# Signs of weights on another engine, first stores from another queue, the seven-product first layer one unit earlier

## The chip, the cores and the metric

The kernel runs on one core of a Trainium2 chip. The metric is device time in microseconds (us) of one execution. The engines are the tensor engine (PE, with its weight loads as PEld), the vector engine (DVE), the scalar engine (ACT), GpSimd (POOL) and the sync engine (SP), which here only issues DMA transfers.

## The reference

Four batches of 768 tokens go through an attention of 8 heads with 64 columns each. A token sees the 96 tokens up to itself and the first 8 of its batch, with a bias that falls with the distance by a slope of the head. Its result, 3072 tokens of 512 columns, goes through two dense layers with a PReLU between them:

```python
scores = scale * (q @ k.T) + bias          # per head
scores = where(is_global | is_local, scores, -1e9)
a = softmax(scores)                        # rows sum to 1
x = (a @ v) -> 3072 x 512                  # heads side by side
h = x @ w_in                               # 512 -> 2048
g = maximum(h, 0) + alpha * minimum(h, 0)
out = g @ w_out                            # 2048 -> 512
```

## The kernel before

The 3072 tokens are 12 units u of 256 tokens (`NU`, `UT`), three to a batch. The 2048 hidden columns are 16 blocks f of 128 (`NF`). All dense products have f32 accuracy from f16 pairs: each operand is a high part and a rest, and three matmuls (high x high, high x rest, rest x high) replace one.

*Weights.* They come as 64-bit floats. `split_w` (L464 to 492) turns each of the 16 blocks, in two parts of 512 columns (of `w_in` and of `w_out`), into f32 and then into an f16 pair. Per part: ACT scales the high word by 2^-112 into `wf`, which moves the exponent (L473, by the helper `mul`, L343); DVE shifts that left by 3 into `wb` (L479); DVE takes the sign bit from the raw word and joins it (L482); DVE joins the top bits of the low word into `wf` (L485); ACT writes the f16 high part (L488), DVE the rest (L363).

*Attention* (`attend`). Scores are 64-row matmuls, softmax is on DVE and ACT. Units 0 and 1 run in plain f32 with PE transposes; from unit 2 on transposes go through DMA, and from unit 4 on (`QU`) the scores are f16 products as well, for which `scale_bias` (L554) rescales the 8 bias tiles `D` on ACT.

*First layer.* `ff_in2` (L853) serves units under `US`: for each block 12 matmuls of 256 columns (L876, 4 column blocks times 3), a scaling by alpha (`g`, ACT, L343), and for each two blocks the maximum on DVE (L885), the f16 high part on ACT (L887) and the rest on DVE (L362). `ff_in4` (L780) serves units from `US` on, for four blocks at a time: a 2x2 scheme of seven instead of eight block products, each 12 matmuls of 128 columns for each of two column halves, into three banks X, Y and Z (L809). ACT takes intermediate sums out of the banks (L817), DVE joins them (L820, L837), applies PReLU (L845) and writes the rest (L362), ACT the high part (L852). It needs four sums of input blocks per unit (`x_combine`, L743, in the names `t` and `xs`) and sums of weights (`combine_w`, L495, in the names `ws` and `sw`).

*Second layer.* `ff_out` (L890) adds block f with three matmuls of 512 columns for each of the two 128-token tiles t (L907). After f = 15 ACT evacuates the tile into `os` (L918) and SP stores it. `os` lies in the tag `stage`, which has two buffers. The two tiles of unit 1 are accumulated in the banks of the tags `sp` and `ax`, which the attention needs too.

*Order.* Every operation has a key (16 slots per unit, L945 to 980) and one or two engines that could do it. A planner (`Plan`, L140) simulates all engines with costs from simple formulas, gives each operation to an engine and writes one queue per engine; tags with a few buffers limit how far it runs ahead. So one changed number moves operations everywhere. The engines execute their queues strictly in order.

A last branch to a general path is taken only for inputs outside the checked bounds; it doesn't run here. Squares of inputs and weights (`energy`, L432) feed that check.

## Time and profile before

| | |
|---|---|
| median of three runs | 608.42 us (608.40 to 608.44) |
| profiled execution | 608.45 us |
| its span in the trace | 606.7 us, 1.75 us less than its time |
| PE busy | 589.6 us, 97% |
| DVE busy | 508.4 us, 84% |
| ACT busy | 409.5 us, 68% |
| mean granted clock of PE | 0.993 |

The span runs from the first instruction to the last. A busy time counts every stretch in which the engine works on some instruction. Instructions of one engine overlap a little at their ends, so the distance of two starts says more of a price than one duration does. The granted clock is a share of 2.4 GHz.

### The profile page before, as it was taken

How to read it: one execution, taken by the hardware profiler on the slowest of the kernel's cores; microseconds unless marked ns; L12 is line 12 of the kernel's file. 1: busy time of each engine (PE TensorE's matmuls, PEld its weight loads, DVE VectorE, ACT ScalarE, POOL GpSimd, SP SyncE). 2: the span in 40 equal slices, each digit the busy share in tenths (PEclk: the TensorE clock that was granted, in tenths of full speed). 3: DMA queues.
4: the chain of work that ended last, by engine and by line, in shares of the span. 5: the costliest groups of instructions: out<-in, count | busy, mean ns of one | idle time of the engine just before them, and what ended most of it. 6: DMA issues, size and time to landing. Idle time of an engine off the chain costs nothing.

```text
span 606.7 us, 15901 instructions
## 1 busy us (share of the span) xinstructions
PE 589.6 (97%) x6218; PEld 416.1 (69%) x6218; DVE 508.4 (84%) x1367; ACT 409.5 (68%) x1088; POOL 1.6 (0%) x11
## 2 busy tenths in 40 slices
PE   8999999998999899999999999999999999999995
PEld 6776576656656666777777777777777777776772
DVE  7999999998999998899889879879788788764531
ACT  7986787885666756869579679668477677542421
POOL 1000000000000000000000000000000000000000
PEclk9999999998999999999999999999999999999998
DMA  8996233347525344557558748648847627313001
GB/s 314 412 409 219 96 111 102 68 119 178 136 76 138 100 119 108 151 117 141 134 96 152 144 97 145 139 80 142 131 107 151 156 66 115 90 27 44 37 1 40
DMA packets 133938, 78.97 MB, mean 130 GB/s; under 512 B 114912, under 2 KB 116960, under 8 KB 133856
## 3 DMA queue, kind: packets, MB, share of 16 engines
q1 hardware_dynamic: 133568, 77.63, 52.4%
q8 instruction: 50, 0.82, 0.6%
q14 instruction: 32, 0.26, 0.1%
q10 hardware_dynamic: 288, 0.26, 0.1%
HBM read 43.79 MB, written 6.29 MB: 83 GB/s over the span
## 4 chain that ended last, share of the span: by engine, by line
PE 75%; DVE 19%; ACT 3%; issue 2%; DMA 1%; ACTq 0%; DVEq 0%
PE o L907 33%; PE hx L809 14%; PE hy L809 7%; PE h L876 7%; PE av L691 4%; PE hz L809 4%; PE sp L610 3%; PE sp L617 2%; DVE g L885 2%; DVE pr L633 2%; DVE gg L362 2%; DVE wf L485 1%; DVE whl L363 1%; DVE wb L482 1%; ACT pr L638 1%
## 5 line engine op out<-in xcount | busy, mean ns | idle before, releaser
L907 PE MATMUL o<-whl,ghl 128*128 128x512 f16 (+1 forms) x774 | 193.8, 378 | 0.0
L809 PEld LDWEIGHTS <-sw 128*128 128x128 f16 x1536 | 93.4, 98 | 20.8
L638 ACT ACTIVATE pr<-pr,sm 128x256 f32<-128x256 f32 (+1 forms) x192 | 92.5, 484 | 20.7 <-DVE sm L633 20.7
L907 PEld LDWEIGHTS <-ghl 128*128 128x128 f16 x774 | 67.1, 98 | 55.2 <-issue 5.1
L876 PE MATMUL h<-xt,whl 128*128 128x256 f16 x768 | 93.2, 276 | 4.5 <-ACT g L343 3.2
L907 PE MATMUL o<-whl,gg 128*128 128x512 f16 x384 | 92.8, 380 | 1.6 <-DVE gg L362 1.3
L876 PEld LDWEIGHTS <-whl 128*128 128x128 f16 x768 | 75.0, 99 | 23.8 <-issue 7.3
L809 PEld LDWEIGHTS <-whl 128*128 128x128 f16 x1152 | 71.0, 98 | 18.9 <-issue 0.2
L633 DVE CUSTOM_DVE_ANT_0 pr<-sp,D 128x256 f32<-128x256 f32 (+1 forms) x192 | 70.1, 397 | 12.0 <-PE sp L610 10.8
L817 ACT ACTIVATE g<-hx 128x256 f32<-128x256 f32 x96 | 36.5, 380 | 59.9 <-PE hx L809 59.6
L845 DVE SCALAR_TENSOR_TENSOR hs<-hs,alpha 128x256 f32<-128x256 f32 x128 | 58.4, 480 | 18.1 <-ACT hs L817 17.3
L907 PEld LDWEIGHTS <-gg 128*128 128x128 f16 x384 | 35.2, 98 | 41.4 <-DVE gg L362 5.1
L363 DVE SCALAR_TENSOR_TENSOR ps<-pr,ps 128x512 f16<-128x512 f32 (+1 forms) x80 | 51.2, 644 | 5.9 <-ACT ps L343 5.7
L362 DVE TENSOR_TENSOR ghl<-hs,ghl 128x512 f16<-128x512 f32 x64 | 42.1, 686 | 2.2 <-ACT ghl L852 2.1
L852 ACT CAST ghl<-hs 128x512 f16<-128x512 f32 x64 | 36.8, 611 | 2.4 <-DVE hs L845 2.4
L638 ACT ACTIVATION_READ_ACCUMULATOR pr<-pr,sm 128x1 f32 x192 | 36.6, 190 | 0.0
L343 ACT ACTIVATE ps<-pr 128x512 f16<-128x512 f32 (+1 forms) x58 | 34.8, 600 | 0.9
L343 ACT ACTIVATE g<-h,ak 128x256 f32<-128x256 f32 x58 | 27.0, 466 | 10.8 <-PE h L876 9.9
L691 PEld LDWEIGHTS <-vp 128*128 128x128 f16 x888 | 30.4, 98 | 3.1 <-issue 0.4
L691 PE MATMUL av<-vp 128*128 128x64 f16 x888 | 32.4, 193 | 0.0
L817 ACT ACTIVATE hs<-hx 128x256 f32<-128x256 f32 x32 | 12.1, 379 | 29.1 <-PE hx L809 29.0
L363 DVE SCALAR_TENSOR_TENSOR vp<-v,vp 128x256 f16<-128x256 f32 (+1 forms) x80 | 31.3, 397 | 0.0
(134 smaller groups left out, 860.4 us busy)
## 6 DMA issues: line engine op xcount, KB each, us to landing
w<-in_w_dram SPq DMA_DIRECT2D x32, 512.0 KB, 8.5
qk<-in_qk_dram SPq DMA_DIRECT2D x28, 336.0 KB, 3.6
v<-in_vw_dram SPq DMA_DIRECT2D x28, 256.0 KB, 3.6
out_dram<-os SPq DMA_DIRECT2D x22, 256.0 KB, 3.5
qk<-in_qk_dram SPq DMA_DIRECT2D x12, 272.0 KB, 3.0
v<-in_vw_dram SPq DMA_DIRECT2D x12, 192.0 KB, 3.3
first<-in_first_dram SPq DMA_DIRECT2D x4, 464.0 KB, 4.7
first<-in_first_dram SPq DMA_DIRECT2D x4, 336.0 KB, 10.0
```

The source lines that it names most:

```text
L343: lambda: nc.scalar.mul(out=out(), in_=src(), mul=by.t if tile_ else by)),
L362: return e.tensor_tensor(out=out(), in0=src(), in1=hi(), op=ALU.subtract)
L363: return e.scalar_tensor_tensor(out=out(), in0=src(), scalar=val(), in1=hi(), op0=ALU.mult, op1=ALU.subtract)
L633: op("DVE", key, c_dve(n) + 10, lambda qb=qb, n=n, dc=dc, pc=pc: v.tensor_tensor_reduce(out=pr.t[:, pc : pc + n], in0=sp.t[:, pc : pc + n] ...
L638: op("ACT", key + 1, c_act(n, ptr=1) + 93, lambda qb=qb, n=n, pc=pc: nc.scalar.activation(out=pr.t[:, pc : pc + n], in_=pr.t[:, pc : pc + ...
L691: nc.tensor.matmul(out, lhsT=p_[:, 128 * j : 128 * j + 128], rhs=v_[:, 64 * j : 64 * j + 64], start=m == 0, stop=m == len(ps) - 1)
L809: nc.tensor.matmul(bank.t[:, 128 * q : 128 * q + 128], lhsT=wt(q, wi, c), rhs=xp(xi, c), start=begin and q == n == 0, stop=n == 5, skip_gr ...
L817: op("ACT", k, c_act(UT, True), lambda: nc.scalar.mul(out=out(), in_=two(bank), mul=KG), r=[bank], w=w, spare=SPARE if u < NU - 1 else 0)
L845: op("DVE", ks[4 + 2 * i], c_dve(UT, ptr=True), lambda n=n: v.scalar_tensor_tensor(out=hs.t[:, n, :], in0=hs.t[:, n, :], scalar=alpha[:, 4 ...
L852: op("ACT", ks[6], c_act(512), lambda q=q, cols=cols: nc.scalar.copy(out=ghl.t[:, 0, cols], in_=flat(q)), r=src, w=[(ghl, q)])
L876: nc.tensor.matmul(hp.t[:, cols], lhsT=w.t[:, wi, wc], rhs=x.t[:, NC * xi + c, :], start=n == 0, stop=n == 3 * NC - 1)
L907: nc.tensor.matmul(o.t[:, cols], lhsT=g_()[:, tok], rhs=w.t[:, wi, 512 + cols.start : 512 + cols.stop], start=f == 0 and n == 0, stop=f == ...
```

## The change

The diff below is whole. In words:

- `US` is 3 instead of 4: unit 3's first layer runs through `ff_in4` and its input through `x_combine`.
- For f from `SIGN` = 6 on, ACT makes the signs: it scales the raw high word once more by 2^-112 into f16, written to every second half-word of a buffer of zeros (`sg`, two of them in the tag `qs`, zeroed once by POOL). What is left of a scaled number at f16 is its sign. DVE then shifts `wf` left and joins `sg` in one instruction, so that the separate shift (L479) goes. For f under 6 the old instructions stay, with the second one writing to `wf`.
- Squares of inputs go to a buffer of the tag `pt` instead of `stage`.
- The 8 bias scalings are spread over slots instead of standing at one.
- The stores of units 0 and 1 are issued by ACT instead of SP.
- In the last unit and block only the second tile is cut into two halves.

```diff
--- before.py
+++ after.py
@@ -307,8 +307,9 @@
 WL = 3
 WLEAD = 8
 WARM = 9
-US = 4
+US = 3
 QU = 4
+SIGN = 6
 QLEAD = 2
 EV = 2
 SLEAD = 36
@@ -429,9 +430,9 @@
 
         en = cn["energies"]
 
-        def energy(key, src, r, col, n):
-
-            t = buf("gg" if n == 512 else "stage", f"sq{col}", [P, n], F16)
+        def energy(key, src, r, col, n, tag="stage"):
+
+            t = buf("gg" if n == 512 else tag, f"sq{col}", [P, n], F16)
             op("ACT", key, c_act(n) + 190, lambda: nc.scalar.activation(
                 out=t.t, in_=src(), func=AF.Square, accum_out=en[:, col : col + 1]), r=r, w=[t, (EN, col)])
 
@@ -455,6 +456,14 @@
             op("PE", key, 150, lambda: nc.tensor.matmul(
                 row.t[:, :NE], lhsT=cn["ones"], rhs=en, start=True, stop=True), r=[EN], w=[row])
             op("DVE", key, 1500, lambda: cn["check"](row.t[:, :NE]), r=[row])
+
+        signs = []
+
+        def clear_signs(key):
+            for i in range(2):
+                x = buf("qs", f"sg{i}", [P, 1344], F16)
+                op("POOL", key, 1500, lambda x=x: nc.gpsimd.memset(x.t, 0.0), w=[x])
+                signs.append(x)
 
         def load_w(f, key):
             raww[f] = [buf(raw_tag(), f"w{f}_{part}", [P, 1024]) for part in range(2)]
@@ -468,7 +477,7 @@
             n = 512
             for part, raw in enumerate(raww[f]):
                 w = buf("wf", f"wf{f}_{part}", [P, n])
-                bits = buf("wb", f"wb{f}_{part}", [P, n], I32)
+                sg = signs[(2 * f + part) % len(signs)]
                 cols = slice(n * part, n * part + n)
                 words = lambda raw=raw: raw.t.bitcast(I32).rearrange("p (n t) -> p n t", t=2)
                 lo_ = lambda words=words: words()[:, :, 0]
@@ -476,15 +485,24 @@
                 k = key + 0.01 * part
                 by = (WI, WO)[part]
                 mul(k, lambda w=w: w.t, lambda hi_=hi_: hi_().bitcast(F32), 2.0**-112, [raw], [w], n=n)
-                op("DVE", k, c_dve(n, True), lambda w=w, bits=bits: v.tensor_scalar(
-                    out=bits.t, in0=w.t.bitcast(I32), scalar1=3, scalar2=None, op0=ALU.logical_shift_left),
-                    r=[w], w=[bits])
-                op("DVE", k, c_dve(n), lambda bits=bits, hi_=hi_: v.scalar_tensor_tensor(
-                    out=bits.t, in0=hi_(), scalar=-0x80000000, in1=bits.t, op0=ALU.bitwise_and,
-                    op1=ALU.bitwise_or), r=[raw], w=[bits])
-                op("DVE", k, c_dve(n), lambda w=w, bits=bits, lo_=lo_: v.scalar_tensor_tensor(
-                    out=w.t.bitcast(I32), in0=lo_(), scalar=29, in1=bits.t, op0=ALU.logical_shift_right,
-                    op1=ALU.bitwise_or), r=[raw, bits], w=[w])
+                if f < SIGN:
+                    bits = buf("wb", f"wb{f}_{part}", [P, n], I32)
+                    op("DVE", k, c_dve(n, True), lambda w=w, bits=bits: v.tensor_scalar(
+                        out=bits.t, in0=w.t.bitcast(I32), scalar1=3, scalar2=None, op0=ALU.logical_shift_left),
+                        r=[w], w=[bits])
+                    op("DVE", k, c_dve(n), lambda w=w, bits=bits, hi_=hi_: v.scalar_tensor_tensor(
+                        out=w.t.bitcast(I32), in0=hi_(), scalar=-0x80000000, in1=bits.t, op0=ALU.bitwise_and,
+                        op1=ALU.bitwise_or), r=[raw, bits], w=[w])
+                else:
+                    op("ACT", k, c_act(n), lambda sg=sg, hi_=hi_: nc.scalar.mul(
+                        out=sg.t[:, : 2 * n].rearrange("p (n t) -> p n t", t=2)[:, :, 1], in_=hi_().bitcast(F32), mul=2.0**-112),
+                        r=[raw], w=[sg])
+                    op("DVE", k, c_dve(n), lambda w=w, sg=sg: v.scalar_tensor_tensor(
+                        out=w.t.bitcast(I32), in0=w.t.bitcast(I32), scalar=3, in1=sg.t[:, : 2 * n].bitcast(I32),
+                        op0=ALU.logical_shift_left, op1=ALU.bitwise_or), r=[sg], w=[w])
+                op("DVE", k, c_dve(n), lambda w=w, lo_=lo_: v.scalar_tensor_tensor(
+                    out=w.t.bitcast(I32), in0=lo_(), scalar=29, in1=w.t.bitcast(I32), op0=ALU.logical_shift_right,
+                    op1=ALU.bitwise_or), r=[raw], w=[w])
                 op("ACT", k, c_act(n), lambda w=w, by=by, cols=cols: nc.scalar.mul(
                     out=out.t[:, 0, cols], in_=w.t, mul=by), r=[w], w=[(out, part)])
                 rest(k, lambda cols=cols: out.t[:, 1, cols], lambda w=w: w.t, by,
@@ -738,7 +756,7 @@
                  [(y, 2 + qb)], 512)
 
         def x_energy(u, key):
-            energy(key, lambda: xt[u].t[:, :NC, :].rearrange("p c t -> p (c t)"), [xt[u], (whl[NF - 1], 3)], 2 * NF + u, 1024)
+            energy(key, lambda: xt[u].t[:, :NC, :].rearrange("p c t -> p (c t)"), [xt[u], (whl[NF - 1], 3)], 2 * NF + u, 1024, "pt")
 
         def x_combine(u, key):
 
@@ -894,7 +912,7 @@
                 acc[u] = [buf(("sp", "ax")[t] if u == 1 else "o", f"o{u}_{t}", [P, 512]) for t in range(2)]
             for t in range(2):
                 o = acc[u][t]
-                parts_ = 2 if u == NU - 1 and f == NF - 1 else 1
+                parts_ = 2 if t and u == NU - 1 and f == NF - 1 else 1
                 n_ = 512 // parts_
                 s = buf("stage", f"os{u}_{t}", [P, 512]) if f == NF - 1 else None
                 rows = u * UT + 128 * t
@@ -920,7 +938,7 @@
                     else:
                         op("DVE", key, c_dve(n_), lambda o=o, s=s, cols=cols: v.tensor_scalar(
                             out=s.t[:, cols], in0=o.t[:, cols], scalar1=OSC, scalar2=None, op0=ALU.mult), r=r, w=[z])
-                    on = nc.scalar if parts_ > 1 and part == 0 else nc.sync
+                    on = nc.scalar if u < 2 or parts_ > 1 and part == 0 else nc.sync
                     store = lambda on=on, s=s, rows=rows, cols=cols: on.dma_start(
                         out=a["out"][rows : rows + 128, cols], in_=s.t[:, cols])
                     if on is nc.sync:
@@ -947,12 +965,12 @@
         def begin(u):
             return 16 * u - LEAD - 2 if u > 2 else (-LEAD0, -LEAD1, 32 - LEAD2)[u]
 
-        jobs = [(-100, build_bias, ()), (-100, warm, ()), (slot(NU - 1, 6), check, ())]
+        jobs = [(-99, clear_signs, ()), (-100, build_bias, ()), (-100, warm, ()), (slot(NU - 1, 6), check, ())]
         for h in range(0, H, 2):
             jobs.append((-90, load_first, (0, h)))
             jobs.append((-60 + h / 8 if h else -71, load_first, (1, h)))
         for h in range(H):
-            jobs.append((begin(QU) - 0.5, scale_bias, (h,)))
+            jobs.append((begin(QU) + 2 * h - 3, scale_bias, (h,)))
         for u in range(NU):
             for h in range(H):
                 jobs.append((begin(u) + (2 if u else 1) * h, attend, (u, h)))
```

Three places show how the queues move. The rows are an engine's queue in order, with line, operation, output and inputs; the numbers behind a name are unit, part and a buffer's running number.

The first place is ACT's queue where the weights of blocks 7 to 9 are split, at about 60 us; before:

```order
L343 ACTIVATE wf7_0_905<-w7_0_480 128x512
L488 ACTIVATE whl5_881<-wf5_1_782 128x512
L343 ACTIVATE g1_1_889<-h1_1_861,ak_153 128x256
L343 ACTIVATE wf7_1_938<-w7_1_554 128x512
L488 ACTIVATE whl6_941<-wf6_0_824 128x512
L343 ACTIVATE g0_2_850<-h0_2_826,ak_153 128x256
L343 ACTIVATE wf8_0_958<-w8_0_614 128x512
L887 CAST gg0_2_961<-g0_2_850 128x512
L887 CAST gg1_1_977<-g1_1_889 128x512
L488 ACTIVATE whl6_941<-wf6_1_859 128x512
L343 ACTIVATE g0_3_998<-h0_3_963,ak_153 128x256
L343 ACTIVATE wf8_1_1007<-w8_1_470 128x512
```

and now, where L344 is the old L343, L506 the old L488 and L497 the new sign:

```order
L344 ACTIVATE wf7_1_927<-w7_1_558 128x512
L497 ACTIVATE sg0_182<-w7_0_484 128x512
L497 ACTIVATE sg1_202<-w7_1_558 128x512
L506 ACTIVATE whl6_948<-wf6_0_835 128x512
L344 ACTIVATE g0_2_878<-h0_2_844,ak_153 128x256
L506 ACTIVATE whl6_948<-wf6_1_880 128x512
L344 ACTIVATE wf8_0_966<-w8_0_618 128x512
L905 CAST gg0_2_969<-g0_2_878 128x512
L905 CAST gg1_1_985<-g1_1_887 128x512
L344 ACTIVATE wf8_1_988<-w8_1_474 128x512
L344 ACTIVATE g0_3_1004<-h0_3_971,ak_153 128x256
L497 ACTIVATE sg0_182<-w8_0_618 128x512
```

Each block has two instructions more on ACT, which stand next to the scalings of the same block or a few places behind them, in front of high parts and evacuations of other blocks.

The second place is SP's queue of transfers at the end of units 0 and 1, at about 137 us (`out_0_dram<-os` is a store, `xt2` unit 2's input for its first layer); before:

```order
L677 DMA_TRANSPOSE vp3_2_1909<-ps3_2_1875 128x6x128
L578 DMA v3_6_1927<-in_vw_dram 128x384
L924 DMA out_0_dram<-os0_0_1949 128x512
L723 DMA_TRANSPOSE xt2_1968<-xs2_0_1951 128x8x128
L723 DMA_TRANSPOSE xt2_1968<-xs2_1_1956 128x8x128
L677 DMA_TRANSPOSE vp3_3_1912<-ps3_3_1920 128x6x128
L575 DMA qk4_0_2003<-in_qk_dram 128x672
L578 DMA v4_0_2005<-in_vw_dram 128x512
L924 DMA out_0_dram<-os0_1_1978 128x512
L924 DMA out_0_dram<-os1_0_1988 128x512
```

and now, where L741 is the old L723:

```order
L596 DMA v3_6_1874<-in_vw_dram 128x384
L593 DMA qk3_6_1891<-in_qk_dram 128x544
L741 DMA_TRANSPOSE xt2_1905<-xs2_0_1877 128x8x128
L741 DMA_TRANSPOSE xt2_1905<-xs2_1_1894 128x8x128
L695 DMA_TRANSPOSE vp3_3_1864<-ps3_3_1936 128x6x128
L596 DMA v4_0_1979<-in_vw_dram 128x512
L593 DMA qk4_0_2038<-in_qk_dram 128x672
```

and in ACT's queue now, where L936 is the evacuation and L942 the store:

```order
L936 ACTIVATE os0_0_1961<-o0_0_676 128x512
L942 DMA out_0_dram<-os0_0_1961 128x512
L936 ACTIVATE os0_1_1971<-o0_1_685 128x512
L942 DMA out_0_dram<-os0_1_1971 128x512
L936 ACTIVATE os1_0_1990<-o1_0_917 128x512
L942 DMA out_0_dram<-os1_0_1990 128x512
L936 ACTIVATE os1_1_2010<-o1_1_923 128x512
L942 DMA out_0_dram<-os1_1_2010 128x512
L352 CAST sw1_2014<-ws1_1973 128x512
L344 ACTIVATE g2_0_2023<-h2_0_1996,ak_153 128x256
```

The stores are gone from SP and stand in ACT's queue, each right behind its evacuation; unit 2's two transposes have loads of attention input in front of them and no store.

The third place is DVE's queue at the start of unit 3's first layer, at about 200 us; before:

```order
L885 SCALAR_TENSOR_TENSOR g3_0_2666<-h3_0_2641,g3_0_2666 128x512
L363 SCALAR_TENSOR_TENSOR ps4_4_2766<-pr4_4_2718,ps4_4_2766 128x512
L363 SCALAR_TENSOR_TENSOR ps4_5_2786<-pr4_5_2727,ps4_5_2786 128x512
L362 TENSOR_TENSOR gg3_0_2789<-g3_0_2666,gg3_0_2789 128x512
L885 SCALAR_TENSOR_TENSOR g3_1_2784<-h3_1_2752,g3_1_2784 128x512
L363 SCALAR_TENSOR_TENSOR vp4_6_2832<-v4_6_2540,vp4_6_2832 128x256
L702 TENSOR_TENSOR xn4_2845<-av4_0_2612,sm4_0_2361 128x2x256
L362 TENSOR_TENSOR gg3_1_2839<-g3_1_2784,gg3_1_2839 128x512
L363 SCALAR_TENSOR_TENSOR vp4_7_2835<-v4_6_2540,vp4_7_2835 128x256
```

and now, where L838 is the join, L863 the PReLU, L520 to 529 the sums of weights:

```order
L838 SCALAR_TENSOR_TENSOR hs3_0_2764<-hz3_0_2727,g3_0_0_2672 128x2x128
L520 TENSOR_TENSOR ws5_2768<-whl10_1247 128x512
L520 TENSOR_TENSOR ws5_2768<-whl11_1348 128x512
L526 TENSOR_TENSOR ws5_2768<-ws5_2768 128x256
L527 TENSOR_TENSOR ws5_2768<-ws5_2768 128x256
L528 TENSOR_TENSOR ws5_2768<-ws5_2768 128x256
L529 TENSOR_TENSOR ws5_2768<-ws5_2768 128x256
L364 SCALAR_TENSOR_TENSOR vp4_6_2828<-v4_6_2545,vp4_6_2828 128x256
L838 SCALAR_TENSOR_TENSOR hs3_0_2764<-hy3_0_2751,g3_0_0_2672 128x2x128
L353 CAST sw5_2845<-ws5_2768 128x512
L863 SCALAR_TENSOR_TENSOR hs3_0_2764<-hs3_0_2764,alpha_65 128x256
L363 TENSOR_TENSOR sw5_2845<-ws5_2768,sw5_2845 128x512
```

A maximum and a rest per two blocks gave way to joins and PReLUs per group of four, and sums of weights stand between them that unit 3 itself needs.

## Rows read from the trace of the kernel before

**Rows 1.** Page, parts 1 and 4: engines' busy time; the chain by engine.

```profile
PE 589.6 (97%) x6218; PEld 416.1 (69%) x6218; DVE 508.4 (84%) x1367; ACT 409.5 (68%) x1088; POOL 1.6 (0%) x11
...
PE 75%; DVE 19%; ACT 3%; issue 2%; DMA 1%; ACTq 0%; DVEq 0%
```

**Rows 2.** Stages: us, busy us (instructions) of each engine, granted clock, DMA share, GB/s.

```profile
20.00:40.00 20.00, 18.72 (x153) 15.43 (x152) 19.73 (x57) 18.05 (x49) 0.00 (x0) 1.00 1.03 416
140.00:160.00 20.00, 18.38 (x132) 12.11 (x131) 17.33 (x51) 13.99 (x38) 0.00 (x0) 0.91 0.70 170
220.00:240.00 20.00, 19.22 (x159) 12.62 (x157) 17.20 (x43) 12.78 (x33) 0.00 (x0) 1.00 0.47 114
240.00:260.00 20.00, 20.00 (x303) 15.74 (x302) 18.33 (x56) 16.36 (x50) 0.00 (x0) 1.00 0.61 159
```

**Rows 3.** Two more stretches in the same columns.

```profile
60.00:130.00 70.00, 69.43 (x496) 45.14 (x495) 69.97 (x165) 54.64 (x127) 0.00 (x0) 1.00 0.35 97
146.00:148.00 2.00, 2.00 (x11) 1.42 (x10) 0.63 (x2) 0.00 (x0) 0.00 (x0) 0.50 1.04 341
```

**Rows 4.** Timeline at 136 to 144 us: start, length, engine, instruction, idle before and releaser.

```profile
136.49 0.60 ACT L918 ACTIVATE os<-o 128x512 f32<-128x512 f32 x1 [0.40 <-PE o L907]
...
137.12 0.35 SPq L924 DMA_DIRECT2D out_dram<-os  x1
...
138.14 3.90 SPq L723 DMA_TRANSPOSE xt<-xs  x2
...
141.73 0.60 ACT L918 ACTIVATE os<-o 128x512 f32<-128x512 f32 x1 [2.08 <-DMA out_dram<-os]
...
142.38 0.92 PE L617 MATMUL sp<-qk 64*128 64x128 f32 x4 [1.22 <-ACT os L918]
...
143.63 0.39 PE L876 MATMUL h<-xt,whl 128*128 128x256 f16 x2 [0.33 <-DMA xt<-xs]
```

**Rows 5.** Pieces of the chain of waits: start, length, engine, work, instructions.

```profile
125.38 1.31 PE h L876 x12
...
250.24 1.34 PE hx L809 x24
```

**Rows 6.** Timeline of DVE from 253 us.

```profile
253.47 0.48 DVE L845 SCALAR_TENSOR_TENSOR hs<-hs,alpha 128x256 f32<-128x256 f32 x1
253.86 0.42 DVE L820 SCALAR_TENSOR_TENSOR hs<-hz,g 128x256 f32<-128x256 f32 x1
254.20 0.68 DVE L362 TENSOR_TENSOR ghl<-hs,ghl 128x512 f16<-128x512 f32 x1
254.80 0.42 DVE L344 TENSOR_SCALAR ps<-pr 128x512 f16<-128x512 f32 x1
```

**Rows 7.** Timeline of ACT and DVE from 75 us.

```profile
75.24 1.29 ACT L343 ACTIVATE wf<-w 128x512 f32<-128x512 f32 x2 [0.82 <-DVE whl L363]
...
76.44 0.49 ACT L638 ACTIVATE pr<-pr,sm 128x256 f32<-128x256 f32 x1
...
77.02 0.76 DVE L479 TENSOR_SCALAR wb<-wf 128x512 int32<-128x512 int32 x2
...
77.69 1.29 DVE L482 SCALAR_TENSOR_TENSOR wb<-w,wb 128x512 int32<-128x512 int32 x2
```

**Rows 8.** Timeline at 242 to 244 us.

```profile
242.14 0.69 DVE L362 TENSOR_TENSOR gg<-g,gg 128x512 f16<-128x512 f32 x1
...
244.11 1.46 PE L907 MATMUL o<-whl,gg 128*128 128x512 f16 x6
```

**Rows 9.** Waits of ACT from 60 to 130 us: total, times, longest.

```profile
ACT wf L343 <- DVE whl L363: 4.4, 9, 0.8
```

**Rows 10.** Timeline of the start.

```profile
0.73 0.20 POOL masks.py:197 MEMSET ident<- 128x128 f32 x1 [0.29 <-POOLq L1135]
...
1.88 0.29 POOL L399 TENSOR_SCALAR_AFFINE_SELECT rel<-rel 128x128 f32<-128x128 f32 x1
...
5.11 1.44 DVE L344 TENSOR_SCALAR D<-D 128x384 bf16<-128x384 f32 x5
```


## Prediction

> **What bounds the kernel now.** I read the page's shares and its chain of waits first, then the table of stages, then the timeline where a stage stands out. The shares put the tensor engine (PE) at 589.6 of 606.7 us, and the chain gives PE 75% and DVE 19% [rows 1]. An average hides that the program has two halves. In the stages the DVE has 19.73 of 20 us from 20 to 40 us already, while PE is short by 1.3; from 240 us on PE has 20.00 of 20 and DVE is loose [rows 2]. So up to 240 us two engines are full together, and behind it only matmul columns count. The stretch 60 to 130 us shows it most sharply: DVE 69.97 of 70, PE 69.43, ACT only 54.64 [rows 3]. Work taken from DVE there can return at most the 0.57 us that PE lacks, as long as PE has the same columns to do.
>
> The one stage that loses much is 140 to 160 us: PE 18.38 of 20, and a granted clock of 0.91 [rows 2]. That is 1.62 us without a matmul and 20 x 0.09 = 1.8 us of clock, 3.4 us together; from 146 to 148 us the clock stands at 0.50, the 1.2 GHz level [rows 3]. The timeline tells why. ACT ends the evacuation of os0_0 at 136.49 + 0.60 = 137.09 and its store is issued at 137.12; ACT's third evacuation waits 2.08 us for it and starts at 141.73, so the store took about 4.6 us. The score matmuls need the bank that this evacuation frees and start at 142.38, after 1.22 us of waiting; the transposes of unit 2's input, issued behind that store at 138.14 and 3.90 us long, then hold the first-layer matmuls until 143.63 [rows 4]. After these gaps the clock falls.
>
> **The change part by part.** Sums are made against the profiled execution: 606.7 us of span and 1.75 us around it, 608.45 us, 0.03 above the median 608.42.
>
> *Unit 3 by seven products, PE.* A chain piece of 12 matmuls of 256 columns takes 1.31 us, one of 24 of 128 columns 1.34 us [rows 5]: 0.109 and 0.056 us each. The plain first layer of one unit has 16 x 12 = 192 matmuls, 20.96 us; the seven products have 4 x 7 x 12 = 336, 18.76 us. That is 2.2 us less on an engine that is full from 240 us to its end. It counts whole as long as DVE hands out unit 3's results no later than PE wants them; rival 3 is the case where it doesn't. Term: -2.2.
>
> *Unit 3, DVE and ACT.* An engine's price for one instruction is read from the starts of two in a row, since ends overlap the next start. DVE starts a 256-wide PReLU at 253.47, a 256-wide join at 253.86, a 512-wide rest at 254.20 and the next at 254.80: 0.39, 0.34 and 0.60 us [rows 6]. Two fast shifts run from 77.02 to 77.69, 0.335 each, two of ACT's scalings of split words from 75.24 to 76.44, 0.60 each [rows 7]. Old unit 3 on DVE: 8 f-pairs x (0.60 + 0.60) = 9.6 us. New: 4 x (4 x 0.39 + 3 x 0.34 + 2 x 0.60) = 15.1 us, and four sums of its input, 4 x 0.34 = 1.4: +6.9. The order gives 16 scalings and casts less to DVE and 6 more to it, priced like the shift: -10 x 0.335 = -3.4. So DVE has 3.5 us more outside the weights, nearly all after 140 us. Its idle time there, 20 - 17.33 and 20 - 17.20 in two stages [rows 2], is 5.5 us and can hold it. At the end of the old unit 3 the last DVE result of the first layer comes at 242.14 + 0.69 = 242.83, and the tensor engine takes it up at 244.11 [rows 8], 1.3 us of slack. I take 0, with ends -1.0 (DVE is early and takes PE's gaps after 200 us with it) and +3.5 (none of its idle time is usable). ACT has 20 takes more, 13 scalings by alpha less and 14 scalings and casts that DVE gave up: 21 x at most 0.60 = 12.6 us over five stages with 6.0 (20 - 13.99) and 7.2 (20 - 12.78) us idle in two of them [rows 2]: 0. The weight sums keep their keys and are needed 16 slots sooner; no row shows that wait. It is bounded by 0 and one sum's DVE work, 2 x 0.60 + 4 x 0.34 + 2 x 0.60 = 3.8 us, and I take 0, because the first products of a group use plain weights and the order has each sum in front of its group.
>
> *Signs from f = 6 on.* 20 parts lose one shift: 20 x 0.335 = -6.7 us on DVE between about 50 and 130 us. ACT gains 20 instructions. None like it is in the trace (every second half-word is written); the nearest is ACT's scaling of the same words, 0.60 [rows 7], which I take: 12.0 us. As ends I set a half and the double of it, 6 and 24 us. ACT has 70 - 54.64 = 15.4 us idle in the stretch 60 to 130 us [rows 3], the largest part of it, 4.4 us, in waits for the weights' rest on DVE [rows 9]. 3.4 us would be left. The instructions have the raw weights alone as input and can go where ACT waits; but behind each sign in ACT's queue stand evacuations that PE needs. By the 0.57 us above, DVE's 6.7 us return little at once: they become lead, which pays for the 3.5 us of unit 3. Term: 0, with ends -0.6 and the rival below.
>
> *Stores of units 0 and 1 from ACT, and the order around them.* SP issues the two transposes with no store ahead of them now, and PE has the first 12 matmuls of unit 2 in front of the score matmuls: 1.31 us of work in the gap of 1.22 us. But the buffers are still two, so ACT's third evacuation still waits for the first store to land, and unit 2's first evacuation stands behind it. Half of the 3.4 us is my value: -1.7, ends 0 and -3.4.
>
> The Trainium skill, "DMA: Bandwidth & Descriptors", section "Issuing engines are not separate DMA queues", says that transfers started by different engines run on the same 16 DMA engines, and that another issuer saves only the time to start them. The trace agrees so far: SP issued this store within 0.03 us of the evacuation's end [rows 4]. By that rule alone this edit is worth 0.
>
> *Zeroed buffers.* Two fills of 1344 elements on POOL at the start. POOL's fill of 128 columns took 0.20 us and its last instruction ends at 1.88 + 0.29 = 2.17 [rows 10]. By columns the two take at most 2 x 10.5 x 0.20 = 4.2 us and would end by 6.4. DVE's five scalings start at 5.11 [rows 10], and the first softmax reads what they write. Ends 0 and +1.3; I take 0, since a fill ten times as wide need not cost ten times as much.
>
> The Trainium skill, "SBUF — State Buffer", section "Who interferes with whom", has DVE's two-port forms (scalings among them) and GpSimd lock each other out for a whole instruction. No row of this trace has the two at once; by that rule the end +1.3 holds if the fills last that long.
>
> *The rest.* Squares in another buffer and the bias scalings spread over slots are the same instructions at other places; the last unit's first tile is evacuated in one piece while the second, unchanged, sets the end: 0, at most +-0.3.
>
> Sum: 608.45 - 2.2 - 1.7 = 604.55; predicted 604.5 us, its own range 603.3 to 605.8.
>
> **Rivals.**
> 1. *The store still lands late.* ACT waits the same 2.08 us, PE runs dry one step later, and the clock falls again. For it: the store was issued without delay and still took 4.6 us. Against: the 12 matmuls and the free SP queue. 608.45 - 2.2 = 606.2. Chance 0.15.
> 2. *Everything is given back.* The stall is gone whole and DVE's lead closes 1.0 us of PE's gaps after 200 us: 608.45 - 2.2 - 3.4 - 1.0 = 601.8. For it: DVE is at 20 of 20 in front of the stall, so lead carries far. Against: in 60 to 130 us PE itself is full. Chance 0.18.
> 3. *Unit 3's DVE work meets the full DVE.* Half of the 3.5 us is not hidden: 608.45 - 2.2 + 1.8 = 608.1, with no store gain left, since PE then waits for DVE anyway. For it: 200 us and later DVE sets the pace. Against: 5.5 us of idle time. Chance 0.12.
> 4. *ACT becomes the bound between 60 and 130 us, and the kernel is slower.* ACT must lose all but 3.4 of its 15.4 us of waits. Each is a hand-over from DVE in a fixed order, and a sign can stand in front of a scaling or an evacuation that is due. If half stay, 7.7 us, the stretch grows by 4.3: 608.45 - 2.2 + 4.3 = 610.6, and at the double price of a sign, with no wait kept, by 8.6: 614.9. From 6.8 us of waits kept on (3.4 + 2.2 + 1.2) it is slower than before. For it: the largest, 4.4 us [rows 9], hangs on the order of DVE's queue and less on its load. Against: signs need nothing but raw weights, and DVE's results come sooner. Chance 0.11.
> 5. *The fills hold up the scalings* at the start: main case + 1.3 = 605.8. Chance 0.04.
>
> Main case: 0.40.
>
> **How the numbers follow.** Within 0.2% (1.2 us) a measurement of this kernel can't be told from no change; that band is 607.2 to 609.6. The main case, rivals 1, 2 and 5 lie below it: 0.40 + 0.15 + 0.18 + 0.04 = 0.77; 0.02 of it goes over for their upper tails, so faster 0.75. Rival 3 and those tails, same 0.14. Rival 4, slower 0.11. The range takes the main case, rivals 1, 3 and 5 and two thirds of rival 2, down to 601.0, up to 608.3: 0.83, less the tails 0.8.
>
> **What would show it.** Unit 3's first layer in 128-column matmuls with no gap of PE over 1 us before them: the -2.2 is right. Near 140 us: PE's idle time under 0.8 us and a granted clock of 1.00 in every stage, or rivals 1 and 2 decide. Between 60 and 130 us ACT at 67 of 70, DVE at 64 to 67 and PE still over 69; PE under 67 and waits of PE for ACT would be rival 4. PE waits for DVE between 200 and 240 us of more than 4 us would be rival 3. The five scalings ending after 6.8 us would be rival 5. I am wrong in the main if PE's columns are not what ends last behind 240 us, or if the sign on ACT takes well over 0.60 us.

## The result, and the profile after

The changed kernel takes 615.29 us (median of 6 runs, 612.87 to 621.64) against 608.41 for the kernel before, run alongside: ratio of the means 1.0138, 95% interval 1.0103 to 1.0172, slower. Its runs spread more than those of before, and the mean granted clock goes with the time (0.992 in the fastest, 0.976 in the slowest); the profiled one, 620.12 us with a span of 618.3, is the second slowest, at 0.978, so its profile has more loss of clock in it than a median run.

The page of the changed kernel, parts 1, 2 (clock of PE in 40 slices) and 4:

```profile
PE 594.1 (96%) x6359; PEld 421.9 (68%) x6359; DVE 508.8 (82%) x1363; ACT 425.8 (69%) x1123; POOL 3.9 (1%) x13
...
PEclk8699999998999999899999999999999999999998
...
PE 77%; DVE 15%; ACT 2%; DMA 2%; issue 2%; ACTq 0%; DVEq 0%; SPq 0%
```

Against [rows 1] POOL has 2.3 us more, and the chain moved 4 points away from DVE, 2 of them to PE. The stages of the changed kernel, in the columns of [rows 2]:

```profile
0.00:20.00 20.00, 16.01 (x86) 12.38 (x87) 13.26 (x60) 11.47 (x40) 3.92 (x13) 0.79 0.91 337
20.00:40.00 20.00, 18.89 (x144) 17.43 (x144) 17.27 (x53) 15.63 (x43) 0.00 (x0) 0.87 1.00 392
...
60.00:80.00 20.00, 20.00 (x131) 13.01 (x130) 19.95 (x38) 18.79 (x39) 0.00 (x0) 1.00 0.43 148
...
140.00:160.00 20.00, 17.59 (x142) 11.46 (x139) 16.18 (x41) 11.81 (x33) 0.00 (x0) 0.91 0.64 148
...
240.00:260.00 20.00, 16.06 (x212) 11.98 (x210) 16.38 (x46) 12.09 (x35) 0.00 (x0) 0.91 0.69 152
```

Three stretches lose: the first 40 us (clock 0.79 and 0.87), 140 to 160 us as before, and 240 to 260 us, where before PE was full. A way to cut the time into parts without trusting busy shares is to take the start of the same work in each kernel: the first matmul of unit 0's first layer, and one product of unit 6. One row each, first for before, then for the changed kernel (instruction, count, lengths in ns, first and last start in us):

```profile
L876 PE MATMUL h<-xt,whl x768: 269/273/421, 26.3 to 238.5; 128*128 128x256 f16 x192
...
L809 PE MATMUL hx<-xt6b,sw x48: 219/219/220, 335.0 to 370.6; 128*128 128x128 f16 x48
```

```profile
L894 PE MATMUL h<-xt,whl x576: 269/273/418, 33.8 to 193.1; 128*128 128x256 f16 x192
...
L827 PE MATMUL hx<-xt6b,sw x48: 219/219/220, 344.6 to 380.2; 128*128 128x128 f16 x48
```

Start, 26.3 to 33.8: +7.5. Middle, from there to unit 6: 335.0 - 26.3 = 308.7 before, 344.6 - 33.8 = 310.8 now: +2.1. Tail, from there to the span's end: 606.7 - 335.0 = 271.7 and 618.3 - 344.6 = 273.7: +2.0. Together the 11.6 us between the spans, each from one profiled run. The tail's 2.0 us lie behind the last evacuation, before and then changed kernel:

```profile
600.27 0.42 DVE L921 TENSOR_SCALAR os<-o 128x256 f32<-128x256 f32 x1 [0.47 <-ACT os L918]
```

```profile
609.97 0.42 DVE L939 TENSOR_SCALAR os<-o 128x256 f32<-128x256 f32 x1 [5.31 <-ACT os L936]
```

It ends at 600.69 and 610.39, 6.0 and 7.9 us before the end of the span. The parts of the start and the middle have their place in the timeline.

The start, changed kernel (the answer to [rows 10]):

```profile
2.11 2.38 POOL L465 MEMSET sg<- 128x1344 f16 x2
2.40 2.11 DVE L1124 CAST nf<-ni 128x4 f32<-128x4 int32 x1 [1.40 <-DMA ni<-in_n_dram]
...
6.79 1.43 DVE L345 TENSOR_SCALAR D<-D 128x384 bf16<-128x384 f32 x5
...
9.38 0.33 PE L676 MATMUL tp<-ident,pr 128*128 128x128 f32 x1 [2.02 <-ACT pr L656]
```

The fills run from 2.11 to 4.49. DVE's cast of four columns, free to start at 2.40, ends with the second of them, after 2.11 us. The five scalings start 1.7 us later than before and PE idles 2.02 us; after that gap the clock falls to 0.50 (1.2 GHz) from about 12 to 24 us in this run.

Around 145 us, changed kernel (the answer to [rows 4]):

```profile
143.12 0.60 ACT L936 ACTIVATE os<-o 128x512 f32<-128x512 f32 x1 [0.24 <-PE o L925]
...
143.75 0.38 ACTq L942 DMA_DIRECT2D out_dram<-os  x1
...
146.49 0.60 ACT L936 ACTIVATE os<-o 128x512 f32<-128x512 f32 x1 [1.71 <-DMA out_dram<-os]
...
148.86 0.60 ACT L936 ACTIVATE os<-o 128x512 f32<-128x512 f32 x1 [1.77 <-DMA out_dram<-os]
...
150.91 5.32 PE L894 MATMUL h<-xt,whl 128*128 128x256 f16 x32 [2.42 <-ACT g L344]
```

ACT now stands twice before buffers that its own stores hold, and unit 2's first scaling, behind both, makes PE wait 2.42 us. Around 245 us, at the end of unit 3:

```profile
243.30 0.38 SPq L593 DMA_DIRECT2D qk<-in_qk_dram  x1
...
247.74 0.66 ACT L344 ACTIVATE qs<-qk 128x544 f16<-128x544 f32 x1 [2.90 <-DMA qk<-in_qk_dram]
248.31 0.37 ACT L835 ACTIVATE hs<-hx 128x256 f32<-128x256 f32 x1
...
248.72 0.83 PE L827 MATMUL hy<-xt,sw 128*128 128x128 f16 x12 [2.85 <-ACT hs L835]
```

ACT waits 2.90 us for unit 6's q and k; the take that empties PE's bank is next in its queue. Both gaps are followed by a fall of the clock (0.91 in both stages). What rival 4 feared didn't come: from 60 to 80 us ACT has 18.79 of 20 and PE is full, over 60 to 130 us ACT has 64.30, DVE 69.86 and PE 70.00 of 70, and the wait of [rows 9] has shrunk:

```profile
ACT wf L344 <- DVE whl L364: 1.3, 3, 0.6
```

### The profile page after: what moved, and what is told of

The parts are those of the page before. It is cut to its first block, busy times and chain, and to the rows that moved or that the text cites. A ratio compares the mean times of both kernels' runs of the same rounds, so it can differ in the third digit from the quotient of the medians.

```text
span 618.3 us, 16212 instructions
## 1 busy us (share of the span) xinstructions
PE 594.1 (96%) x6359; PEld 421.9 (68%) x6359; DVE 508.8 (82%) x1363; ACT 425.8 (69%) x1123; POOL 3.9 (1%) x13
## 4 chain that ended last, share of the span: by engine, by line
PE 77%; DVE 15%; ACT 2%; DMA 2%; issue 2%; ACTq 0%; DVEq 0%; SPq 0%
PE o L925 34%; PE hx L827 14%; PE h L894 8%; PE hy L827 7%; PE av L709 5%; PE hz L827 3%; PE sp L635 3%; PE sp L628 3%; DVE pr L651 2%; DVE ps L364 1%; PE tp L676 1%; DVE ws L520 1%; DMA xt<-xs 1%; DVE hs L863 1%; DMA qk<-in_qk_dram 1%
## 5 line engine op out<-in xcount | busy, mean ns | idle before, releaser
L925 PE MATMUL o<-whl,ghl 128*128 128x512 f16 x867 | 218.8, 380 | 0.5 <-DVE ghl L363 0.4
L827 PEld LDWEIGHTS <-sw 128*128 128x128 f16 x1728 | 105.3, 98 | 27.1 <-issue 4.7
L925 PEld LDWEIGHTS <-ghl 128*128 128x128 f16 x867 | 75.4, 98 | 64.2 <-issue 5.5
L827 PEld LDWEIGHTS <-whl 128*128 128x128 f16 x1296 | 80.2, 98 | 22.5 <-issue 2.2
L863 DVE SCALAR_TENSOR_TENSOR hs<-hs,alpha 128x256 f32<-128x256 f32 x144 | 65.8, 479 | 18.6 <-ACT hs L835 17.7
L894 PE MATMUL h<-xt,whl 128*128 128x256 f16 x576 | 70.7, 277 | 4.3 <-ACT g L344 3.5
L925 PE MATMUL o<-whl,gg 128*128 128x512 f16 x288 | 67.8, 379 | 0.8 <-DVE gg L363 0.7
L894 PEld LDWEIGHTS <-whl 128*128 128x128 f16 x576 | 55.9, 99 | 18.4 <-issue 7.6
L363 DVE TENSOR_TENSOR ghl<-hs,ghl 128x512 f16<-128x512 f32 x72 | 47.3, 684 | 2.2 <-ACT ghl L870 2.1
L925 PEld LDWEIGHTS <-gg 128*128 128x128 f16 x288 | 27.0, 98 | 31.5 <-DVE gg L363 3.5
L344 ACT ACTIVATE ps<-pr 128x512 f16<-128x512 f32 (+1 forms) x65 | 38.9, 598 | 1.6 <-DMA vp<-ps 0.6
L827 PE MATMUL hy<-xt,sw 128*128 128x128 f16 x432 | 30.0, 219 | 2.9 <-ACT hs L835 2.9
```

What stands on the lines that cost most here:

```text
L344: lambda: nc.scalar.mul(out=out(), in_=src(), mul=by.t if tile_ else by)),
L363: return e.tensor_tensor(out=out(), in0=src(), in1=hi(), op=ALU.subtract)
L827: nc.tensor.matmul(bank.t[:, 128 * q : 128 * q + 128], lhsT=wt(q, wi, c), rhs=xp(xi, c), start=begin and q == n == 0, stop=n == 5, skip_gr ...
L863: op("DVE", ks[4 + 2 * i], c_dve(UT, ptr=True), lambda n=n: v.scalar_tensor_tensor(out=hs.t[:, n, :], in0=hs.t[:, n, :], scalar=alpha[:, 4 ...
L894: nc.tensor.matmul(hp.t[:, cols], lhsT=w.t[:, wi, wc], rhs=x.t[:, NC * xi + c, :], start=n == 0, stop=n == 3 * NC - 1)
L925: nc.tensor.matmul(o.t[:, cols], lhsT=g_()[:, tok], rhs=w.t[:, wi, 512 + cols.start : 512 + cols.stop], start=f == 0 and n == 0, stop=f == ...
```

## The experiments

Ratios are of the means, against the kernel before, run alongside. "Start" is the start of unit 0's first layer, "middle" the distance from there to unit 6's product, "tail" the rest of the span; they are read from one profiled run each, so a difference of clock between two such runs is part of them.

**x1: fills only.** Queues of all engines but POOL as before.

```diff
+        jobs: (-99, clear_signs, ())   # two gpsimd.memset(sg, 0.0), read by nobody
```

> The kernel before with the two POOL fills of 1344 half-words at the start and nothing else; nobody reads what they fill, and every queue but POOL's is word for word that of before. Theory A (the fills lock DVE out of its first cast, the bias comes 1.7 us late, PE runs dry and its clock falls to 1.2 GHz): DVE's cast of n at about 2.4 us takes 2.1 us instead of 0.17, PE idles about 2 us near 8 us, and the time is 2 to 8 us above before (610.4 to 616.4). Rival B (the start doesn't matter, since DVE and PE catch up; the loss lies in queues from 140 us on): within 1.2 us of 608.4.

Ratio 1.0083 (1.0048 to 1.0117). Eight runs of one program lie between 608.46 us (granted clock 0.999) and 617.37 (0.982). The profiled one:

```profile
2.41 2.09 DVE L1111 CAST nf<-ni 128x4 f32<-128x4 int32 x1 [1.41 <-DMA ni<-in_n_dram]
```

```profile
L881 PE MATMUL h<-xt,whl x768: 269/273/418, 35.2 to 247.5; 128*128 128x256 f16 x192
...
L814 PE MATMUL hx<-xt6b,sw x48: 219/219/220, 343.9 to 379.6; 128*128 128x128 f16 x48
```

Start +8.9, middle 308.7 as before to the tenth, tail 271.7 as before. So the fills alone cost what the start lost, and nothing is caught up later (rival B falls). That the size hangs on the clock is read from the mean clocks of the eight runs; this one alone has a profile, and x3 below is a second case.

**x2: fills by DVE**, in the changed kernel, while it waits for n.

```diff
-                op("POOL", key, 1500, lambda x=x: nc.gpsimd.memset(x.t, 0.0), w=[x])
+            v.memset(x.t.bitcast(F32), 0.0)      # 672 words, before the cast of n
```

> The changed kernel with the two fills made by DVE (672 words each) while it waits for the transfer of n, before its first cast; POOL fills nothing. Theory A: DVE's bias starts as early as in the kernel before, the granted clock is 1.00 from 0 to 40 us, and the time falls by 2 to 8 us from the changed kernel's 615.3, to 607 to 613. Rival B: the start changes but the time stays at 614 to 617.

Ratio 1.0086 (1.0068 to 1.0104); 612.1 us, runs 610.14 to 613.81. The two fills take 1.33 us, the scalings start at 4.92, unit 0's first layer at 26.1 and the clock is 1.00 up to 240 us. Theory A holds for the start, and the rest stays slower than before: PE waits 1.83 us at 141 us as in the changed kernel, the clock falls at 240 us, and the tail is 273.6. Middle 334.7 - 26.1 = 308.6.

**x3: stores of units 0 and 1 from SP**, in the changed kernel, POOL fills kept.

```diff
-                    on = nc.scalar if u < 2 or parts_ > 1 and part == 0 else nc.sync
+                    on = nc.scalar if parts_ > 1 and part == 0 else nc.sync
```

> The changed kernel with the stores of units 0 and 1 issued by SP again; the queues differ in few places else. Theory A leaves 614 to 617, since the start is the same. Theory C (ACT's queue is held twice, 1.7 and 1.8 us, by stores that it issued itself, and unit 2's first evacuation stands behind them): the gap of PE of 2.4 us near 150 us is gone and the time falls by 1 to 3 us, to 612 to 614. The Trainium skill's rule that the issuer doesn't matter would leave ACT's waits as they are.

Ratio 1.0027 (1.0004 to 1.005), runs 606.73 to 614.74: more than theory C asked. The middle is 305.2 against 310.8 (first layer from 28.0, unit 6 at 333.2). Its profiled run had the late start without a fall of the clock. More than the issuer differs, though: some 70 rows of ACT's queue and some 120 of DVE's stand at other places. Unit 2's first scaling now stands in front of ACT's third evacuation, which waits only 0.19 us:

```profile
143.20 0.47 ACT L344 ACTIVATE g<-h,ak 128x256 f32<-128x256 f32 x1 [0.23 <-PE h L894]
...
143.86 1.24 ACT L936 ACTIVATE os<-o 128x512 f32<-128x512 f32 x2 [0.19 <-DMA out_dram<-os]
```

**x4: unit 3 by seven products and nothing else**, on the kernel before (`US = 3`).

> The kernel before with the seven products from unit 3 on and nothing else (signs on DVE, stores from SP, no fills). Theory D (unit 3's extra work on DVE and the load of q and k that ACT waits for near 245 us belong to the seven products in unit 3): slower than before by 2 to 6 us, 610 to 614, with PE gaps between 200 and 260 us. Theory A: the columns' saving shows, 605 to 608.

Ratio 1.0112 (1.0092 to 1.0133): slower, theory D. Middle 341.6 - 28.8 = 312.8, 4.1 more than before, with PE short by 2.1 and 1.9 us in the stages 200 to 240 and by 3.5 from 240 to 260, where the clock is 0.91. Its start is late too (28.8), without any fills: PE waits 1.91 us for a transfer, and the clock falls:

```profile
8.12 1.57 PE L617 MATMUL sp<-first 64*128 64x128 f32 x8 [1.91 <-DMA first<-in_first_dram]
```

**x5: fills by DVE and stores from SP** (x2 and x3 together).

> The changed kernel with both found causes undone: fills by DVE while it waits, stores of units 0 and 1 from SP; signs and unit 3 as changed. Against before in the same runs: if start and stores were the whole loss, 1 to 3 us faster (ratio 0.995 to 0.998), with the granted clock at 1.00 up to 140 us. If the wait of ACT for unit 6's q and k (2.8 us of PE near 238 us) also counts, only 0 to 1 us faster or the same.

Ratio 0.9981 (0.9968 to 0.9994). Middle 305.7. With both causes out the rest of the change is 1.1 us faster than before, between the two expectations; the wait for unit 6's q and k is still there.

**x6: x5, and unit 6's scaling of q and k behind the takes.** The planner is told that this load takes longer.

```diff
-                op("SP", kp - 4, ..., w=[x])
+                op("SP", kp - 4, ..., w=[x], spare=2500 if u == 6 and h == 0 else 0)
```

> As the run before, and unit 6's first scaling of q and k moved about ten places back in ACT's queue (the planner is told that this one load takes 2.5 us more); 14 rows of ACT's queue differ. Theory E (ACT stands 2.8 us in front of a load, and the take that PE waits for stands behind it): PE's gap of 2.7 us near 238 us goes, and the time falls by 2 to 3.5 us from the run before, to a ratio of 0.990 to 0.994. Rival F (DVE is late there anyway, since unit 3 gives it more to do): the gap stays under another name, and the time within 0.8 us of the run before.

Ratio 0.9954 (0.9937 to 0.9972), 604.64 us, 1.85 less than x5, a little short of theory E's range. But of the 2.1 us between the two profiled spans (604.7 and 602.6) only 0.8 lies in the middle (305.7 and 304.9); the start gives 0.7 and the tail 0.6. So rival F is nearer: the gap comes back under another name. What stands there now:

```profile
239.65 0.63 ACT L344 ACTIVATE ps<-pr 128x512 f16<-128x512 f32 x1 [2.13 <-DMA vp<-ps]
...
241.15 0.83 PE L824 MATMUL hx<-xt4b,sw 128*128 128x128 f16 x12 [1.61 <-ACT g L832]
```

ACT waits for a transpose instead, and PE 1.61 us for a take behind it.

**x7: x5 with unit 3 as before** (`US = 4`): signs and the small edits.

> As x5, with the seven products from unit 4 on as before: what is left of the change is the signs by ACT, squares in another buffer and the spread bias scalings. If signs give DVE lead that PE can use: 0.5 to 2 us faster than before. If PE had no room for it from 60 to 130 us and the stall at 140 us stays: within 0.8 us of before. If ACT pays for it: slower by 1 to 3 us.

Ratio 0.9958 (0.9943 to 0.9972), 604.92 us, a larger gain than any of the three expectations. Middle 328.5 - 26.0 = 302.5, 6.2 less than before; the tail, 273.9, takes 2.2 of it back.

**x8: x4 with the late scaling of x6.**

> The seven products from unit 3 on alone (x4), with unit 6's first scaling of q and k moved back as in x6. Theory E: 3 to 6 us less than x4's ratio of 1.011, to 1.002 to 1.006, since a wait of 2.9 us and a fall of the clock behind it go. Theory D (DVE has too much to do without the signs): PE's gaps between 200 and 240 us stay, and the ratio stays above 1.007.

Ratio 1.0083 (1.006 to 1.0105): theory D. The middle is 1.2 us shorter than x4's (311.6), which is less than the fall of x4's clock from 240 to 260 us is worth (20 x 0.09 = 1.8 us; x8 has none there). The gaps from 200 to 260 us stay.

**x9: x7 with the stores from ACT.**

> x7 (signs by ACT, fills by DVE, unit 3 as before) with the stores of units 0 and 1 issued by ACT. Theory C (ACT waits for the landing of a store that frees one of two buffers, and unit 2's first evacuation stands behind it): slower than x7 by 3 to 6 us, ratio to before 1.001 to 1.006, with a PE gap and a fall of the clock at 140 to 156 us that x7 doesn't have. The rule that the issuer doesn't matter: within 1 us of x7's 0.996.

Ratio 0.9968 (0.9951 to 0.9985), no different from x7 (middle 302.3). Theory C fails as a price that goes with the issuer. ACT's queue there:

```profile
136.88 0.60 ACT L933 ACTIVATE os<-o 128x512 f32<-128x512 f32 x1 [0.24 <-PE o L922]
...
139.02 1.06 ACT L436 ACTIVATE sq<-xt 128x1024 f16<-128x1024 f16 x1 [0.49 <-DMA xt<-xs]
140.25 0.60 ACT L933 ACTIVATE os<-o 128x512 f32<-128x512 f32 x1
...
142.78 0.60 ACT L933 ACTIVATE os<-o 128x512 f32<-128x512 f32 x1 [1.93 <-PE h L891]
```

A square stands between the second and the third evacuation, and by then the first store has landed. In the changed kernel nothing stood there. Here, too, queues differ in more than the issuer.

**x10: the signs alone**, on the kernel before (fills by DVE; squares, bias scalings and last store as before).

> The kernel before with nothing but the signs by ACT from f = 6 (fills by DVE); squares, bias scalings and the last store as before. If the gain of x7 is the signs': ratio 0.994 to 0.998, with the clock at 1.00 from 140 to 160 us. If it comes from the small edits: 0.998 to 1.002.

Ratio 0.9928 (0.9911 to 0.9944), 602.37 us: with x13 the fastest of the complete versions. Middle 302.5 as in x7, so the gain is the signs'. The rest of unit 2's input, which its transposes wait for, ends at 137.43 + 0.68 = 138.11 before and at 131.65 + 0.68 = 132.33 here. From the profile of before, then of x10:

```profile
137.43 0.68 DVE L362 TENSOR_TENSOR xs<-xn,xs 128x512 f16<-128x512 f32 x1
```

```profile
131.65 0.68 DVE L363 TENSOR_TENSOR xs<-xn,xs 128x512 f16<-128x512 f32 x1
...
132.36 4.08 SPq L738 DMA_TRANSPOSE xt<-xs  x2
...
135.72 1.25 ACT L933 ACTIVATE os<-o 128x512 f32<-128x512 f32 x2 [0.24 <-PE o L922]
...
138.76 4.09 PE L891 MATMUL h<-xt,whl 128*128 128x256 f16 x36
```

Counted from the first layer's start (26.0, before 26.3), unit 0's evacuation comes 0.5 us earlier than before, 109.7 against 110.2. But unit 2's transposes are issued at 132.36 instead of 138.14, 5.5 us earlier by this count, and its first layer starts at 112.8 instead of 117.3 and runs 36 matmuls in one piece; the clock is 1.00 from 140 to 160 us.

**x11: x6 with unit 3's PReLU narrowed**, queues as in x6.

```diff
-                        out=hs.t[:, n, :], in0=hs.t[:, n, :], ...
+                        out=hs.t[:, n, :m_], in0=hs.t[:, n, :m_], ...   # m_ = 32 in unit 3
```

> x6 with unit 3's 16 PReLU instructions on 32 of their 256 columns: the other columns of unit 3 keep their value before PReLU. Every queue is in the same order as in x6; DVE has some 4 us less to do between 185 and 240 us. Theory D (DVE sets the pace in unit 3, so that the saved columns of PE return nothing): faster than x6 by 2 to 4 us. Rival (PE waits for ACT's takes or for transfers): within 0.7 us of x6.

Ratio 0.9958 (0.9939 to 0.9976), 603.93 us: by the ratio the same as x6, as the rival has it. But the profile has PE 20.00 instead of 19.12 from 200 to 220 us and a middle of 303.2, 1.7 under x6, in spite of a larger gap behind it (2.18 us): part of the work that came sooner waited at ACT's next transpose.

**x12: signs from f = 3** (`SIGN = 3` in x7).

> x7 with ACT's signs from f = 3 on instead of 6: six shifts less on DVE (2 us) between 25 and 55 us, six instructions more on ACT, which has 18.0 of 20 us there. If DVE's lead is what counts: 0.5 to 2 us faster than x7. If ACT is full there: slower than x7 by 1 to 3 us.

Ratio 0.9958 (0.9936 to 0.9979), as x7. But its tail is 271.4 us against x7's 273.9, and its middle 305.5 against 302.5: in the profiled run the second theory's loss is there and the shorter tail hides it. PE waits for ACT, and from 38 to 40 us the clock is 0.50:

```profile
35.49 0.66 PE L673 MATMUL tp<-ident,pr 128*128 128x128 f32 x4 [1.36 <-ACT pt L677]
```

**x13: x6 with takes in front of the scalings that wait for transposes.**

```diff
-                op("SP", key + 2, 115 * 2 * nb, transposes, r=[ps], w=[rpt])
+                op("SP", key + 2, 115 * 2 * nb + (2000 if u == 5 else 0), transposes, r=[ps], w=[rpt])
```

> x6 with unit 5's score transposes told to the planner as 2 us longer, so that ACT's takes for PE stand in front of the scaling that waits for such a transpose (25 rows of ACT's queue differ). If PE's gap of 1.6 us near 240 us is this wait alone: 1 to 2 us faster than x6, ratio to before 0.992 to 0.994. If DVE sets the pace up to 232 us and the gap returns under another name: within 0.7 us of x6 (0.994 to 0.997).

Ratio 0.9922 (0.9902 to 0.9943), 602.87 us, 1.8 under x6, as the first theory said. This is the change with its fills, stores and two scalings put right, and it is faster than the kernel before. It is no faster than the signs alone (x10, 0.9928, middle 302.5 in both).

**x14: x13 with the narrowed PReLU of x11.**

> x13 with unit 3's 16 PReLU instructions on 32 of 256 columns (the other columns keep their value before PReLU); queues as in x13. If DVE's work and the queue behind transposes are together what eats the saving of the seven products in unit 3: 3 to 5 us faster than x6, ratio 0.987 to 0.991, under x10's 0.993. If something else eats it: not under 0.992.

Ratio 0.9899 (0.9877 to 0.992), 601.45 us, 3.2 under x6. Middles: x6 304.9, x13 302.5, x14 300.9. The two last stages of unit 3, for x6 and then x14:

```profile
200.00:220.00 20.00, 19.12 (x220) 12.92 (x218) 19.76 (x52) 12.22 (x35) 0.00 (x0) 1.00 0.36 81
220.00:240.00 20.00, 17.74 (x204) 11.48 (x203) 19.02 (x52) 16.84 (x47) 0.00 (x0) 1.00 0.62 119
```

```profile
200.00:220.00 20.00, 19.92 (x241) 13.97 (x243) 19.75 (x53) 13.07 (x37) 0.00 (x0) 1.00 0.32 84
220.00:240.00 20.00, 18.93 (x226) 13.11 (x223) 19.05 (x58) 16.90 (x49) 0.00 (x0) 1.00 0.66 121
```

## Why the prediction was wrong

In the profiles the middle goes from before to x7 (signs) by -6.2, from x7 to x3 (unit 3) by +2.7 and from x3 to the changed kernel (stores) by +5.6. The three add up to +2.1 by construction. Other pairs say how firm they are: signs -6.2 again (x10), unit 3 +3.2 (x5 against x7) and +4.1 (x4 against before), stores +2.9 (x2 against x5). Start and tail add 7.5 and 2.0. By the ratios over all runs, in which the tail is included, the stores cost 6.4 to 6.7 us (x2 against x5, changed kernel against x3) and the fills 2.8 to 5.0 (x3 against x5, changed kernel against x2, x1 against before). Only rival 4 forecast a slower kernel, and its mechanism didn't occur. Step by step:

- *Zeroed buffers: "I take 0".* The largest failed step in the profiled run, the second by the ratios. The two fills took 2.38 us where my bound by columns was 4.2, and the end +1.3 was looked for in the scalings at 5.11. They end at 8.22, which is rival 5's sign; but the fills locked the cast at 2.40, an instruction of 0.17 us that heads the chain of the bias. The direct cost is 1.7 us, as x3's start without a fall of the clock has it (28.0 against 26.3; starts without fills and without a fall lie between 26.0 and 27.2). What I left out altogether is the clock: the gap of 2 us is followed by 1.2 GHz in some runs, and the start loses up to 8.9 us (x1). Rival 5, at a chance of 0.04, had the fills and not this size. The Trainium skill's "SBUF — State Buffer", section "Who interferes with whom", says that of a two-port form and GpSimd the one that issues first has the shared ports for the whole instruction and the other "fully blocks". This case's trace agrees with the blocking: the cast ended at 4.51, the fills at 4.49. A hand-over after one instruction it doesn't show: the cast, free from 2.40, ended only with the second fill.
- *Stores: "Half of the 3.4 us is my value: -1.7".* The largest failed step by the ratios, and wrong in sign. I wrote that ACT's third evacuation waits and unit 2's first evacuation stands behind it, and then let the 12 matmuls in front cover it. But the fourth evacuation waits too, 1.71 and 1.77 us, and behind both PE runs dry for 2.42. What decides is the order in ACT's queue and not the issuer: in x3 unit 2's scaling stands in front of the third evacuation, in x9 a square between two evacuations lets ACT's own store land, and the gap is gone in both. That is read from the queues; no run moved the order alone. Of the 5.6 us, 3.5 are there when unit 3's first layer starts (204.1 - 33.8 against 194.7 - 28.0 in x3). Most of the rest is the fall of the clock behind the wait for unit 6's q and k; x3 has the same wait (2.72 us) at full clock, so that part isn't shown to be the stores'. The Trainium skill's "DMA: Bandwidth & Descriptors", section "Issuing engines are not separate DMA queues", lets another issuer save only the time to start a transfer, and by it alone the edit would have been worth 0; x9 against x7 agrees (0.9968 and 0.9958). What neither the rule nor my sum looked at is who stands behind the wait.
- *Signs: "Term: 0, with ends -0.6".* Right for the stretch and wrong for the program. Up to unit 0's evacuation the gain is 0.5 us, as the 0.57 us said; DVE stays at 69.86 of 70, not the 64 to 67 that I looked for. The lead shows where unit 2's input goes out: its first layer starts 4.5 us earlier, and the stage's clock of 1.00 instead of 0.91 is the rest of the 6.2. I had booked this stall under the stores, since the transposes stand behind a store in SP's queue; but they were issued at 138.14, 0.03 us after DVE's last work on their input. Two limits: the clock doesn't fall in every run of before (its mean clock is 0.993 in the profiled run and up to 0.999 in others), and by the ratio of x10 the signs give 4.4 us; and the signs also move the order, which alone can do part of it, since x4 without signs starts unit 2's first layer at 143.56 - 28.8 = 114.8. ACT's 20 signs (0.77 us long, 0.64 from start to start) fitted, as costed: rival 4 fell.
- *Unit 3: "Term: -2.2".* The columns are fewer as worked out, but with signs the unit costs 2.7 to 3.2 more, without them 4.1 (x4). The statement hung on DVE handing out results in time, and the 5.5 us of idle time that I counted as cover lay in the stall and, at unit 3, mostly in one piece from 225 to 230 us (DVE 2.96 of 5). Rival 3 had half of this right: x13 against x14 shows 1.6 us by DVE's PReLUs, and x6 against x13 2.4 us by takes that stand in ACT's queue behind waits for transposes. Its sign, waits for DVE of more than 4 us, isn't met: PE waits 1.4 us for DVE from 200 to 240 us, and 2.85 for ACT just behind. With both away the unit gives 302.5 - 300.9 = 1.6 us, near the 2.2, but x14 leaves out work that the seven products need; the complete x13 gives nothing over x7. That ACT's queue would hold PE there, no step of mine had.
- *The rest: "0, at most +-0.3".* The tail is 2.0 us longer, and nearly all of it lies behind the last evacuation (7.9 against 6.0 us). In the changed kernel, x2, x7 and x9 the tail is 273.4 to 273.9 us, in before and the eleven other runs 271.3 to 272.3, most of them with the same last instructions. In these four alone the queue of instruction loads moved 7 packets in the last 13 us, in the others 6. Here are changed kernel and x5:

```profile
q14 instruction: 7, 0.06, 1.2%
```

```profile
q14 instruction: 6, 0.05, 1.1%
```

That one more load costs the 2 us wasn't tried and stays open; why these four programs have it isn't known. x10 (tail 271.5) is ahead of x7 (273.9) by as much.

## What to carry to other kernels

A few microseconds of fill on an idle engine aren't free when the engine that heads the chain can't work beside it (here a cast took 2.11 us instead of 0.17): give the fill to an engine that waits anyway, and look at what starts during the fill, not after it. Work taken from a full engine pays where its lead is next handed over, so the gain is looked for at the next stall and not in the full stretch itself. Before work moves into an in-order queue, ask for every wait in it what stands behind: PE stood 2.42, 2.85 and 1.61 us here behind ACT's waits for a store, a load and a transpose. Moving the last two waits behind the takes gave back 3.2 us of the middle (x5 to x13), and moving one of them alone 0.8. When two versions tie, compare their stretches one by one: a loss in the middle can hide behind a shorter tail (x12).

## What the hardware showed

A gap of about 2 us of PE near 8 us is followed by very different clocks. One profiled run each:

| | gap of PE | it ended with | mean granted clock, 8 to 28 us | start of the first layer |
|---|---|---|---|---|
| x1, fills | 1.80 us | ACT's `pr` | 0.57 | 35.2 us |
| changed kernel, fills | 2.02 us | ACT's `pr` | 0.66 | 33.8 us |
| x3, fills | 2.07 us | ACT's `pr` | 1.00 | 28.0 us |
| x4, no fills | 1.91 us | a transfer | 0.91 | 28.8 us |

The length of the gap doesn't order them. Eight runs of x1, whose queues are those of before on every engine but POOL, lie between 608.46 us at a mean clock of 0.999 and 617.37 at 0.982. A kernel at this edge can't be judged by one run.
